# A gate store and the o-gate loads at other places in the SyncE queue (mLSTM and two MoE layers, fp32)

## The chip, the cores and the metric

The kernel runs on one core of a Trainium2 chip. The metric is the device time of one execution in microseconds (us), as the median of several runs. "Faster" and "slower" compare that time with the time of the kernel before, on the same chip.

## The reference, cut to what matters

Three layers follow each other. The first is an mLSTM with 2 batches, 8 heads, 768 steps and a head size of 40; its output feeds a top-2 mixture of 8 experts (320 to 1024 to 320), and that feeds a dense layer (320 to 2048 to 320). The change lies in the first.

```python
for t in range(S):
    m_new = np.maximum(f_gate[:, :, t] + m, i_gate[:, :, t])
    f_stab = np.exp(f_gate[:, :, t] + m - m_new)
    i_stab = np.exp(i_gate[:, :, t] - m_new)
    m = m_new
    C = f_stab * C + i_stab * np.einsum('bhd,bhe->bhde', vt, kt)
    n = f_stab * n + i_stab * kt
    h_tilde = np.einsum('bhde,bhe->bhd', C, qt)
    denom = np.maximum(np.abs(nq), 1.0)          # nq = n . q
    o = 1.0 / (1.0 + np.exp(-o_gate[:, :, t]))
    y[:, :, t] = o * h_tilde / denom
x = _moe_ref(y, ...)        # x @ w1[e], relu, @ w2[e], two experts for each row
return _moe2_ref(x, ...)    # h = x @ w_in; (h * cos(h)) @ w_out
```

## The kernel before, in words

**Tiling.** The 768 steps of each batch are cut into 6 chunks of 128 (NC = 6), so the recurrence becomes matmuls inside a chunk and a state handed from chunk to chunk. Twelve steps n = 0 to 11 follow each other in `att_step` (lines 854 to 909): n = 0 to 5 is the first batch, n = 6 to 11 the second. "qk 5" below is the load of step 5. From step 6 on the router and the experts are woven in, and from about 125 us on the program is the experts and the dense layer.

**Gates.** `gates_a(c0, c1)` (line 84) computes running sums of the gates of chunks c0 to c1-1 on VectorE, all 16 heads of both batches at once, into `g_G`, a part of the tile `g_all`. From chunk 2 on the weights of a chunk need these sums broadcast over 128 partitions. That goes through DRAM: `g_G` is stored to `GD` ("gd" in the profile, lines 102 and 103), and `load_gb(n)` (line 170) reads it back into a tile `gb`, the same 4 KB for each of 128 partitions. The sums of chunks 0 to 3 are stored once in `gates_a(2, 4)`, before step 0, and those of chunks 4 and 5 in `gates_a(4, NC)`, which step 1 calls (line 889). The load of `gb` has to wait until the store has landed.

**Loads.** All loads and stores around the change are issued by SyncE (SP), in program order, on one DMA queue; an issue waits on SP until its tile is free and its data are there, and what stands behind it in SP's program waits too. `load_qk(n)` (line 161) brings q and k with two DMAs of 40 partitions each, into one of three tiles, so qk n+3 waits until step n has used its tile up (the last user is `mk_q(n)`, lines 232 to 237, on VectorE for n = 2 and on GpSimd for n = 4 and 5). `load_kv(n)` (line 178) brings k and v, with three tiles too; its tile is free once `mm_out(n-3)` is through. `load_o(i)` (line 152) brings the o-gate of steps 2i and 2i+1 into a tile `ogt`; `tanh_o(i)` (line 156) turns it on ScalarE at the end of step i, and `mk_y` (line 315) uses it in steps 2i and 2i+1.

**Order of one step.** `att_step(n)` runs on TensorE `mm_state(n)`, `mm_out(n)`, `mm_s(n+2)` (line 239, it reads qk n+2) and the router's matmuls of the step before (`rt_a`, `rt_b`, lines 341 to 359); on VectorE `mk_state`, `mk_p(n+1)` and, for some n, `mk_q(n+1)`; then `loads(n+1)` (line 843), `mk_y(n)` with the store of the chunk's result ("xd", line 329), and on ScalarE and GpSimd `mk_w(n+2)` (line 199, it reads `gb`). `loads(n)` asks for qk n+3, gb n+3, kv n+2 and o tile n+1. For n = 2 the two `gb` tiles 4 and 5 stand at its end, since the store of their gates comes only in step 1.

Of the kernel before, what the change touches and what calls it, by code (L numbers as in the profile page):

```python
# [20 lines left out]
C = 128  # L21
NC = S // C
# [18 lines left out]
def tile_mlstm_moe_moe2(ctx, tc, qk, kv, og, gi, gf, wcat, noise, wm1, wm2, cst, out):  # L41
    nc = tc.nc
    V, A, G, T, Y = nc.vector, nc.scalar, nc.gpsimd, nc.tensor, nc.sync
# [13 lines left out]
    def psS():  # L57
        return ps.tile([128, 512], FT, name="pS", tag="S", bufs=3)

    def psM():  # L60
        return ps.tile([128, 512], FT, name="pM", tag="M", bufs=1)
# [3 lines left out]
    g_i, g_f, g_m, g_g, g_G = (g_all[0:16, i, :] for i in range(5))  # L65
# [14 lines left out]
    GD = dr.tile([NC, 16, C], FT, name="gd")  # L80
# [3 lines left out]
    def gates_a(c0, c1):  # L84
        a, z = c0 * C, c1 * C
        s = slice(a, z)
        a1 = max(a, 1)
        if a == 0:
            V.memset(g_g[:, 0:1], 0.0)
        V.tensor_tensor_scan(out=g_m[:, s], data0=g_f[:, s], data1=g_i[:, s],  # L90
                             initial=(-1e30 if a == 0 else g_m[:, a - 1:a]), op0=OP.add, op1=OP.max)
        V.tensor_tensor(out=g_g[:, a1:z], in0=g_f[:, a1:z], in1=g_m[:, a1 - 1:z - 1], op=OP.add)
        V.tensor_tensor(out=g_g[:, a1:z], in0=g_g[:, a1:z], in1=g_m[:, a1:z], op=OP.subtract)
        V.tensor_scalar(g_g[:, a1:z], g_g[:, a1:z], -110.0, None, op0=OP.max)
        for c in range(c0, c1):
            V.tensor_tensor_scan(out=g_G[:, c * C:(c + 1) * C], data0=g_r, data1=g_g[:, c * C:(c + 1) * C],
                                 initial=0.0, op0=OP.mult, op1=OP.add)
        if c0 < 2:
            A.activation(gG[:, s], g_G[:, s], AF.Copy)
        if c0 >= 2:  # L100
            d0 = 0 if c0 == 2 else c0
            Y.dma_start(GD[d0:c1].rearrange("c p t -> p c t"),
                        g_G[:, d0 * C:c1 * C].rearrange("p (c t) -> p c t", t=C))

    def gates_b(c0, c1):
        n = c1 - c0
# [26 lines left out]
    for i in range(NB):  # L133
        t = ap_.tile([128, 4, NH, C], FT, name=f"qk{i}")
# [4 lines left out]
    for i in range(2):  # L139
        t = ap_.tile([128, H, 64], FT, name=f"kb{i}")  # L140
        G.memset(t, 0.0)
        KBS.append(t)
    for i in range(2):
        t = ap_.tile([128, NH, 82], FT, name=f"st{i}")
# [7 lines left out]
    def load_o(i):  # L152
        t = OT[i] = mp.tile([128, 2, KO], FT, name="ogt", tag="wl" if i % 2 else "wh", bufs=4)
        Y.dma_start(t, og[:, 2 * i:2 * i + 2, :])
# [6 lines left out]
    def load_qk(n):  # L161
        if n >= 2 * NC:
            return
        b, c = divmod(n, NC)
        d = L[n]
        t = d["qk"] = QKS[n % NB]
        Y.dma_start(t[0:D, 0:3], qk[b, c, 0])
        Y.dma_start(t[64:64 + D, 1:4], qk[b, c, 1])

    def load_gb(n):  # L170
        if n >= 2 * NC:
            return
        b, c = divmod(n, NC)
        t = L[n]["gb"] = ap_.tile([128, H, C], FT, name="gb", bufs=3)
        Y.dma_start(t, bass.AP(tensor=GD.tensor, offset=GD.offset + (c * 16 + b * H) * C,
                               ap=[[0, 128], [C, H], [1, C]]))

    def load_kv(n):
        if n >= 2 * NC:
            return  # L180
        b, c = divmod(n, NC)
        d = L[n]
        t = ap_.tile([128, KO + H * (D + 1)], FT, name="kv", bufs=NB)
        Y.dma_start(t, kv[b, c])
        d["k"] = t[:, 0:KO].rearrange("p (h d) -> p h d", d=D)
        d["v"] = t[:, KO:].rearrange("p (h d) -> p h d", d=D + 1)
# [630 lines left out]
    load_kv(1)  # L817
    load_qk(2)
    gates_a(0, 1)
    gates_b(0, 1)  # L820
    gates_t(0, 1)
    gates_c(0, 1)
    mm_g(0)
    mk_w(0)
    mm_s(0, (0, 1))
    gates_a(1, 2)
    gates_b(1, 2)
    gates_t(1, 2)
    mm_s(0, (2, 3))
    gates_a(2, 4)  # L830
    gates_c(1, 2)
    mk_e(0)
# [10 lines left out]
    def loads(n):  # L843
        load_qk(n + 3)
        if n > 2 or n == 0:
            load_gb(n + 3)
        load_kv(n + 2)
        if n < 5:
            load_o(n + 1)
        if n == 2:  # L850
            load_gb(4)
            load_gb(5)

    def att_step(n):
        if n == 0:
            loads(0)
# [31 lines left out]
        if n == 1:  # L888
            gates_a(4, NC)
        loads(n + 1)  # L890
        if n == 2 * NC - 1:
            mk_y(n)
# [83 lines left out]
    for g in range(2, NG - 1):  # L976
        n = len(groups[g + 1][1])
# [33 lines left out]
    for q in range(3):  # L1011
        for i in range(3):
            c = 3 * q + 3 + i
# [25 lines left out]
    with tc.If(over > 0):  # L1039
# [9 lines left out]
        for b in range(B):  # L1049
            with tc.For_i(0, NC, 1) as it:  # L1050
# [4 lines left out]
                p = psM()  # L1055
# [6 lines left out]
                for e in range(E):  # L1062
                    acc = psA()
                    for f in range(8):
                        w = mp.tile([128, FW], FT, name="wr", tag="wh", bufs=4)
                        Y.dma_start(w, wm1[e, :, f, :])
                        p = psS()
# [13 lines left out]
                for f in range(16):  # L1081
                    wh, wl = W2[f // 4][:, 0, f % 4, :], W2[f // 4][:, 1, f % 4, :]
                    p = psS()
# [6 lines left out]
                t = mp.tile([128, DM], FT, name="yt", tag="yt", bufs=3)  # L1090
# [76 lines left out]
```

## Time and profile before

| what | us |
|---|---|
| median of 3 runs | 522.38 |
| lowest and highest of the 3 runs | 521.79, 523.95 |
| the profiled execution, its own time | 524.33 |
| its span in the trace | 522.1 |
| TensorE busy in that span | 489.9 (94%) |
| VectorE, ScalarE, GpSimd busy | 367.5, 326.1, 275.4 |
| DMA moved | 76.36 MB, 146 GB/s on the mean |

The span is what the trace shows of one execution, and 2.2 us of the execution's own time lie outside it. Times inside the trace count from the span's start. A share of busy time is a mean over stages that have different limits, so the stretch around the change is read by itself, and the later stages only for what they do with a shift.

### The profile page before, as it was taken

What the parts mean: (1) busy time and instruction counts of PE and PEld (TensorE: products, weight loads), DVE (VectorE), ACT (ScalarE), POOL (GpSimd) and SP (SyncE); (2) the same over time, 40 slices, a digit from 0 to 9 for tenths busy, and PEclk for the clock granted to TensorE, in tenths of its full rate; (3) what the DMA queues carried; (4) which work ended last, traced back from release to release, by engine and by line L of the source; (5) the groups of instructions that cost most, each with busy time, mean ns of one, the idle gap of its engine ahead of it and who ended that gap; (6) DMA issues with size and microseconds to landing.
All of it is one profiled execution on the core that took longest, in us unless ns stands there. A gap on an engine that the chain in (4) does not pass through costs nothing.

```text
span 522.1 us, 9011 instructions
## 1 busy us (share of the span) xinstructions
PE 489.9 (94%) x3198; PEld 470.2 (90%) x3198; DVE 367.5 (70%) x779; ACT 326.1 (62%) x695; POOL 275.4 (53%) x234
## 2 busy tenths in 40 slices
PE   4897998799999999999999997999999999999995
PEld 3796887699999999999999997989999999999995
DVE  8885387568458776868776678688956655687772
ACT  3658567355555454545555465578877777777773
POOL 6435465656846868585868687264366347300000
PEclk9999999799999999999999999999999999999998
DMA  6889785396373927391847384031021003001001
GB/s 182 255 266 268 222 269 172 119 294 261 95 285 134 334 84 268 131 352 59 325 151 254 116 312 163 28 104 26 1 64 52 1 1 102 13 2 38 1 2 43
DMA packets 25396, 76.36 MB, mean 146 GB/s; under 512 B 3872, under 2 KB 11392, under 8 KB 25344
## 3 DMA queue, kind: packets, MB, share of 16 engines
q1 hardware_dynamic: 22752, 67.11, 37.3%
q0 software_dynamic: 2592, 8.61, 5.6%
q8 instruction: 27, 0.44, 0.3%
q14 instruction: 25, 0.20, 0.1%
HBM read 66.47 MB, written 9.22 MB: 145 GB/s over the span
## 4 chain that ended last, share of the span: by engine, by line
PE 73%; DVE 12%; DMA 7%; ACT 3%; issue 3%; POOL 1%; SPq 0%; DVEq 0%; POOLq 0%; ACTq 0%
PE pS L594 34%; PE pA L603 10%; PE pA L600 10%; PE pA L599 10%; DMA qk<-qk 3%; PE pM L555 2%; PE pA L612 1%; PE pA L611 1%; DMA xgt<-xd,idxe 1%; DMA gb<-gd 1%; PE pS L310 1%; PE pA L247 1%; PE pM L355 1%; DVE c_t L717 1%; DMA gd<-g_all 1%
## 5 line engine op out<-in xcount | busy, mean ns | idle before, releaser
L587 POOL TENSOR_TENSOR wl<-wraw,wh 128x704 fp32r<-128x704 f32 x69 | 123.0, 1791 | 61.4 <-ACT wh L585 56.0
L649 DVE SCALAR_TENSOR_TENSOR hb<-pS,hb 128x384 fp32r<-128x384 f32 (+2 forms) x128 | 45.9, 390 | 45.8 <-ACT hb L646 45.0
L585 ACT ACTIVATE wh<-wraw 128x704 fp32r<-128x704 f32 x80 | 62.9, 786 | 14.3 <-PE pA L611 8.2
L594 PE MATMUL pS<-xh,wh 128*128 128x448 f32 (+1 forms) x240 | 69.5, 344 | 0.5 <-ACT xh L557 0.5
L594 PE MATMUL pS<-xh,w 128*128 128x384 f32 x288 | 66.7, 340 | 1.5 <-DVE m_t L758 1.5
L594 PE MATMUL pS<-xh,wl 128*128 128x448 f32 (+1 forms) x240 | 66.2, 330 | 0.4 <-POOL wl L587 0.4
L599 PE MATMUL pA<-wh,hb 128*128 128x320 f32 x208 | 62.3, 309 | 0.0
L600 PE MATMUL pA<-wl,hb 128*128 128x320 f32 x208 | 62.2, 309 | 0.0
L743 ACT ACTIVATE m_t<-pS,magic 128x384 f32<-128x384 f32 x64 | 37.1, 580 | 28.7 <-PE pS L594 28.1
L646 ACT ACTIVATE hb<-pS 128x448 fp32r<-128x448 f32 (+1 forms) x80 | 37.7, 472 | 25.9 <-PE pS L594 19.0
L594 PEld LDWEIGHTS pS<-xh,w 128*128 128x128 f32 x288 | 50.0, 188 | 2.8 <-DVE m_t L758 2.8
L758 DVE SCALAR_TENSOR_TENSOR m_t<-m_t,pS 128x384 f32<-128x384 f32 x64 | 35.4, 553 | 16.7 <-ACT m_t L757 16.1
L603 PE MATMUL pA<-wh,hb 128*128 128x320 f32 x208 | 44.1, 312 | 3.0 <-DVE hb L649 2.9
L594 PEld LDWEIGHTS pS<-xh,wl 128*128 128x128 f32 x240 | 43.2, 190 | 2.7 <-POOL wl L587 0.6
L744 DVE TENSOR_SCALAR m_t<-m_t 128x384 f32<-128x384 f32 x64 | 23.1, 361 | 27.3 <-ACT m_t L743 27.1
L594 PEld LDWEIGHTS pS<-xh,wh 128*128 128x128 f32 x240 | 40.9, 190 | 1.5 <-ACT xh L557 0.6
L764 POOL TENSOR_TENSOR wl<-m_t,wh 128x384 fp32r<-128x384 f32 x25 | 25.4, 1017 | 30.7 <-ACT wh L762 21.4
L594 PE MATMUL pS<-xl,wh 128*128 128x448 f32 (+1 forms) x160 | 39.7, 329 | 0.0
L600 PEld LDWEIGHTS pA<-wl,hb 128*128 128x128 f32 x208 | 38.7, 186 | 0.6
L599 PEld LDWEIGHTS pA<-wh,hb 128*128 128x128 f32 x208 | 38.6, 186 | 0.6
L546 POOL DMA_INDIRECT xgt<-xd,idx x28 | 34.3, 1224 | 7.8 <-DVE idx L519 3.2
L745 DVE SCALAR_TENSOR_TENSOR m_t<-pS,m_t 128x384 f32<-128x384 f32 x64 | 35.7, 558 | 2.2
(201 smaller groups left out, 1243.4 us busy)
## 6 DMA issues: line engine op xcount, KB each, us to landing
wraw<-wm SPq DMA_DIRECT2D x36, 704.0 KB
raw<-wm SPq DMA_DIRECT2D x16, 704.0 KB
qk<-qk SPq DMA_DIRECT2D x24, 240.0 KB
gb<-gd SPq DMA_DIRECT2D x10, 512.0 KB
kv<-kv SPq DMA_DIRECT2D x12, 324.0 KB
yd<-yt SPq DMA_DIRECT2D x22, 160.0 KB
wraw<-wm SPq DMA_DIRECT2D x8, 352.0 KB
ogt<-og SPq DMA_DIRECT2D x6, 320.0 KB
```

Source lines behind the costliest of these rows:

```text
L546: G.indirect_dma_start(out=t[:n, :], out_offset=None, in_=XD[0:S, :] if g < 2 else XD[:, :], in_offset=bass.IndirectOffsetOnAxis(ap=(idxe ...
L585: A.activation(wh, raw[:, f, :], AF.Copy)
L587: eng.tensor_tensor(out=wl, in0=raw[:, f, :], in1=wh.bitcast(FT), op=OP.subtract)
L594: T.matmul(p[:, :n], w[:, 128 * k:128 * k + 128], x[:, m, :], start=(i == 0), stop=(i == 7))
L599: T.matmul(a[:n, :DM], hh[:, s], wh[:, KW:], start=first, stop=False)
L600: T.matmul(a[:n, :DM], hh[:, s], wl[:, KW:], start=False, stop=False)
L603: T.matmul(a[:n, :DM], hl[:, s], wh[:, KW:], start=False, stop=last)
L646: A.activation(hh[:, :n], p[:, :n], AF.Relu)
L649: V.scalar_tensor_tensor(out=hb[:, o:o + z - a], in0=p[:, a:z], scalar=0.0, in1=hh[:, a:z].bitcast(FT), op0=OP.max, op1=OP.subtract)
L743: A.activation(t, m["p"], AF.Identity, bias=magic, scale=0.5 / PI)
L745: V.scalar_tensor_tensor(out=t, in0=m["p"], scalar=0.5 / PI, in1=t, op0=OP.mult, op1=OP.subtract)
L758: V.scalar_tensor_tensor(out=s, in0=s, scalar=1.0, in1=m["p"], op0=OP.subtract, op1=OP.mult)
```

## The change

The store of the gates of chunks 4 and 5 leaves `gates_a` and becomes a function of its own, `gates_d`. `gates_a(2, 4)` still stores chunks 0 to 3 where it did. The other store now stands in `loads(2)`, behind the issues of qk 5, an o tile and kv 4, and right ahead of the loads of gb 4 and gb 5. The o tiles move as well: o tile n is asked for in `loads(n)` and no longer in `loads(n-1)`, and it stands ahead of the kv tile and not behind it.

```diff
         if c0 < 2:
             A.activation(gG[:, s], g_G[:, s], AF.Copy)
-        if c0 >= 2:
-            d0 = 0 if c0 == 2 else c0
-            Y.dma_start(GD[d0:c1].rearrange("c p t -> p c t"),
-                        g_G[:, d0 * C:c1 * C].rearrange("p (c t) -> p c t", t=C))
+        if c0 == 2:
+            gates_d(0, c1)
+
+    def gates_d(c0, c1):
+        Y.dma_start(GD[c0:c1].rearrange("c p t -> p c t"),
+                    g_G[:, c0 * C:c1 * C].rearrange("p (c t) -> p c t", t=C))
...
         load_qk(n + 3)
         if n > 2 or n == 0:
             load_gb(n + 3)
+        if 0 < n < NC:
+            load_o(n)
         load_kv(n + 2)
-        if n < 5:
-            load_o(n + 1)
         if n == 2:
+            gates_d(4, NC)
             load_gb(4)
             load_gb(5)
```

No instruction is added or taken away. Each of the lines stands for one DMA issue on SP (two for a qk).

## Rows read from the trace of the kernel before

**Rows 1.** Chain that ended last, 0 to 75 us: start us, length us, what
```profile
14.13 1.80 DMA gd<-g_all
...
29.07 2.11 DMA gd<-g_all
...
31.24 6.16 DMA gb<-gd
...
43.43 7.77 DMA qk<-qk
```

**Rows 2.** Timelines of ScalarE and TensorE, 13 to 72 us: start, length, what, [idle before]
```profile
37.48 2.45 ACT L209 ACTIVATE wt<-gb,tok 128x128 f32<-128x128 f32 x8 [1.37 <-DMA gb<-gd]
...
42.28 0.94 PE L355 MATMUL pM<-wc,xTt 128*128 128x128 f32 x6 [1.23 <-ACT xTt L348]
...
51.34 1.15 PE L247 MATMUL pA<-qk 128*128 128x256 f32 x2 [2.01 <-DMA qk<-qk]
```

**Rows 3.** Busy time by stretch, 50 to 56 us: PE, PEld, DVE, ACT, POOL, PEclk, DMA share, GB/s
```profile
50.00:52.00 2.00, 0.66 (x2) 0.60 (x3) 1.38 (x4) 2.00 (x9) 0.64 (x1) 0.85 0.96 338
52.00:54.00 2.00, 2.00 (x10) 1.81 (x9) 1.05 (x2) 0.72 (x2) 0.70 (x2) 0.50 1.03 278
54.00:56.00 2.00, 2.00 (x13) 1.86 (x12) 0.00 (x0) 0.00 (x0) 0.66 (x1) 0.80 0.89 239
```

**Rows 4.** The page: busy tenths of TensorE in 40 slices of 13 us
```profile
PE   4897998799999999999999997999999999999995
```

**Rows 5.** Timeline of SP's issues: start, length, line, what
```profile
6.19 0.30 SPq L168 DMA_DIRECT2D qk<-qk  x1
...
29.07 0.34 SPq L102 DMA_DIRECT2D gd<-g_all  x1
29.50 0.31 SPq L167 DMA_DIRECT2D qk<-qk  x1
...
31.24 0.81 SPq L175 DMA_DIRECT2D gb<-gd  x2
```

**Rows 6.** Busy time by stretch, 12 to 36 us, columns as in rows 3
```profile
12.00:14.00 2.00, 1.75 (x4) 0.85 (x3) 1.90 (x5) 0.00 (x0) 0.74 (x1) 1.00 0.66 229
...
26.00:28.00 2.00, 2.00 (x18) 1.95 (x17) 1.90 (x4) 0.49 (x1) 0.69 (x3) 1.00 0.62 190
28.00:30.00 2.00, 2.00 (x19) 1.95 (x18) 1.79 (x6) 1.11 (x5) 0.45 (x1) 1.00 0.52 182
...
34.00:36.00 2.00, 1.73 (x17) 1.54 (x16) 1.50 (x4) 0.34 (x3) 0.46 (x1) 1.00 1.02 375
```

**Rows 7.** DMA issues of the whole run: out<-in, engine, count, KB each
```profile
qk<-qk SPq DMA_DIRECT2D x24, 240.0 KB
gb<-gd SPq DMA_DIRECT2D x10, 512.0 KB
kv<-kv SPq DMA_DIRECT2D x12, 324.0 KB
...
ogt<-og SPq DMA_DIRECT2D x6, 320.0 KB
```

**Rows 8.** Timelines of VectorE and TensorE, step 1: who frees qk 5's and kv 4's tiles
```profile
24.89 0.68 DVE L237 TENSOR_TENSOR qtt<-qk,get 128x512 f32<-128x512 f32 x1
25.48 1.21 DVE L90 TENSOR_TENSOR_SCAN g_all<-g_all 16x256 f32<-16x256 f32 x1
...
28.09 0.95 DVE L96 TENSOR_TENSOR_SCAN g_all<-g_r,g_all 16x128 f32<-16x128 f32 x2
...
27.08 0.61 PE L310 MATMUL pS<-kv,ppt 128*128 128x82 f32 x4
```

**Rows 9.** Timeline of ScalarE: when o tiles 3 and 5 are used, and the idle after tile 4
```profile
45.88 0.72 ACT L157 ACTIVATE ogt<-ogt 128x640 f32<-128x640 f32 x1
...
56.92 0.49 ACT L348 ACTIVATE xTt<-pM 128x384 f32<-128x384 f32 x1 [4.21 <-PE pM L346]
...
61.11 0.73 ACT L157 ACTIVATE ogt<-ogt 128x640 f32<-128x640 f32 x1
```

## The prediction

> **What bounds the kernel now.** I read the chain that ended last first, then the waits of the engines in the stretch that the change touches, then the queue. In the chain, DMA holds four long pieces between 14 and 52 us [rows 1]: two gate stores, the load of gb 4, which lands at 31.24 + 6.16 = 37.40 us, and qk 7, which lands at 43.43 + 7.77 = 51.20 us. The reader is to see that a store of 16 KB needs 2.11 us and one of 32 KB 1.80 us: a small transfer costs its fixed way there and back, about 1.8 us, and hardly its bytes. The loads of 480 to 512 KB take 6 to 8 us; that is not their bytes but what stands ahead of them.
>
> Two of these landings stop engines [rows 2]. ScalarE waits 1.37 us for gb 4, and as its queue runs in order the router's xTt of step 2 comes late behind it: TensorE waits 1.23 us at 42.28. Then TensorE waits 2.01 us for qk 7 at 51.34. Behind that second wait the granted clock falls from 2.4 to 1.2 GHz [rows 3]: the means 0.85, 0.50 and 0.80 over three stretches of 2 us lose 2 x (0.15 + 0.50 + 0.20) = 1.7 us of clock. Together these are 1.23 + 2.01 + 1.7 = 4.9 us, all that a better order of loads could win here. From 125 us on (slice 10) TensorE is busy 9 tenths in nearly every slice [rows 4]: whatever the first stage gains or loses is handed through to the end, with nothing that would take it up.
>
> **Is there room in the queue?** At 26 to 30 us the DMA engines are busy only 0.62 and 0.52 [rows 6], while qk 5 could already be under way: its tile is free at 24.89 + 0.68 = 25.57 and its issue stands at 29.50, behind the gate store, which waits for VectorE's scans until 28.09 + 0.95 = 29.04 [rows 5, 8]. This is what the change goes after. But the share is a mean over 16 engines. At 12 to 14 us the last thing asked for was qk 2, at 6.19 [rows 5], and the 2 x 229 = 458 kB moved then are less than its two halves of 240 KB, 492 kB [rows 6, 7]. So a qk alone keeps 0.66 of the engines busy, 10.6 of 16, and moves 229 GB/s, where gb and kv in the stretch from 34 us get 375. A 0.6 with a qk ahead is therefore a queue whose fullest engines do not rest.
>
> The Trainium skill says the same in two places of "DMA: Bandwidth & Descriptors": under "Why a DMA increments its semaphore by 16 and not by 1", that a DMA is spread over the largest number of engines up to 16 that divides its outer dimension, by which 40 partitions give 10; and under "Queues, rings and completion order", that each engine takes its descriptors in ring order. By that rule the moved store cannot pass the loads that are now ahead of it on those ten engines, and it speaks against this change. The 0.66 agrees with the 10; what the rule makes of the time is the main case below, and the time without it is rival 1.
>
> **The change part by part.**
>
> *The price of each load in the queue.* Of the 1.80 us I give half, 0.9, to the way before the data and half to the way back; no row splits it, so the ends are 0 and 1.8. Then qk 5 (issued 29.50), kv 4, an o tile and gb 4 are served from 30.4 to 36.5, 6.1 us. At 375 GB/s gb (524 kB) is 1.40, kv (332 kB) 0.88, an o tile (328 kB) 0.87; qk is left with 2.95. Its lower bound is 492 kB at 229 GB/s, 2.15.
>
> *The o tiles one step later.* Up to `loads(2)` one o tile less has gone in, so the queue reaches qk 5 0.87 us earlier: 29.5 and not 30.4. From then on each `loads(n)` up to 4 holds one o tile as before, so the lead neither grows nor shrinks; at `loads(5)` the extra tile comes back and costs 0.87 us of the queue. Who uses the tiles: tanh 2 has them long before. Tile 4 has 4.21 us of idle ScalarE behind it [rows 9], so a late one costs nothing unless it is over 4.2 us late. Tiles 3 and 5 are rival 3. The kv tiles now stand 0.87 us later within their step; their users, GpSimd's kb and the next step's matmuls, come a step or more later, and I cost this at nothing, with 0.5 us as the other end.
>
> *The loads ahead of the store.* On SP qk 5 can issue at 25.6, the o tile at 26.3, kv 4 when `mm_out(1)` has let its tile go at 27.08 + 0.61 = 27.7 [rows 8]. All three are issued by about 28.1, so the store still leaves SP at 29.07, as soon as the scans are through; SP's order costs it nothing. The queue does. That a transfer waits for the fullest of its engines I take from gb 4, whose 6.16 us [rows 1] are over what its bytes need by the time of the loads ahead. So the store is served behind 29.5 + 2.95 (qk 5) + 0.87 (o) + 0.88 (kv 4) = 34.2, and with its way back it lands at 35.2 instead of 31.18. The ends are 34.3 and 36.1 by the split of the 1.8 us.
>
> *What waits for the store.* gb 4 leaves SP 0.06 us after the landing, as before (31.18 to 31.24) [rows 1], and nothing is ahead of it in the queue, so it lands 1.80 + 1.40 = 3.2 us after its issue, at 38.45 against 37.40: **+1.05 us**, with +0.1 and +1.9 as ends. Behind it on SP wait gb 5, the store of step 1's result and qk 6, gb 6 and so on. These lose nothing of their own: gb 4 and gb 5 fill the engines until about 39, and qk 6 issues at 36.4.
>
> *The same in terms of the queue.* But for the store itself it is empty from 34.2 to 35.25 + 0.9 = 36.1, some 1.9 us in which nobody asks for anything, and it has 0.87 us less to carry: everything behind, up to qk 8, is 1.9 - 0.87 = +1.0 us. Before, the round trip of the store was covered by qk 5, kv 4 and the o tile issued behind it; now that cover has gone ahead of it.
>
> *To the end.* ScalarE's wait for gb 4 becomes 1.37 + 1.05 = 2.4 us, and TensorE's at 42.28 becomes 2.3. qk 7 is issued a little later, which its place in the queue hides, and lands at 52.2. TensorE was there at 51.34 - 2.01 = 49.33, would now be at 49.33 + 1.05 = 50.4 and wait 1.8 us, so step 5 starts at 52.3 and not 51.34. **Sum: +1.0 us**, 525.3 against the profiled execution's 524.33. That execution was 1.95 us above the median of the runs; on the median the sum gives 522.38 + 1.0 = **523.4 us**.
>
> **The rivals.**
>
> *1. The store is not held up.* If the engines that it uses are not those that are behind, it lands near 31.2 as before. gb 4 then follows kv 4 without a hole: 34.2 + 1.4 + 0.9 = 36.5, 0.9 us earlier, and qk 7 is 0.9 us earlier too. That is 521.5, and if the shorter waits spare the clock, another 1.7 us: 519.8. For it: the mean share of 0.52 to 0.62 at 26 to 30 us. Against: at that share qk's engines are full, and gb 4 took 6.16 us behind qk 5.
>
> *2. The clock falls elsewhere.* TensorE's first wait grows to 2.3 us, over the 2.01 us behind which the clock fell; the second shrinks to 1.8. If it falls behind the first, the slow stretch of 1.7 us lies in step 4, where TensorE has those 1.8 us to wait for qk 7 anyway, and step 5 runs at 2.4 GHz: +1.0 - 1.7 = -0.7, and as qk 9 is late by the extra o tile, some of it is lost again: 521.7 to 522.4. For it: the lengths of the waits. Against: the wait of 1.23 us cost no clock, and one example does not tell where between 1.23 and 2.01 it turns.
>
> *3. An o tile comes too late (slower).* tanh 5 stands in ScalarE's queue at 61.11 [rows 9], in a stretch where ScalarE itself is on the chain; with the shift it is wanted at 62.1. Behind qk 7 (52.2) come gb 7, o 4, kv 6, a result store (160 KB, 0.44), qk 8, gb 8 and o 5: 1.40 + 0.87 + 0.88 + 0.44 + 2.95 + 1.40 + 0.87 = 8.8, landing at 61.0. But from gb 4 to qk 7 the same prices give 11.3 us where the trace has 13.8 [rows 1], a factor of 1.22; with it o 5 lands at 62.9 and tanh 5 waits 0.8 us, with the upper end of gb 4 as much as 1.7. Everything behind it shifts: +1.0 + 0.8 to 1.7, or 524.2 to 525.1. It decides from the point where o 5 lands after 62.1; tile 3 (wanted at 46.9, landing at 45.5 to 47.1) has the same trouble but qk 7's wait hides it.
>
> *4. The parts cancel.* The saved o tile and the hole in the queue are equal (the split of the 1.8 us at its low end): 522.4.
>
> **How the numbers follow.** Main case 0.42; rival 1 0.10; rival 2 0.23; rival 3 0.15; rival 4 0.10. What a measurement of this kernel can tell from no change is about 0.5%, 2.6 us. Of the cases only the better half of rival 1 is faster by that (0.05); rival 3's upper end together with the main case's (+1.9) is slower by it (0.12). The rest, 0.83, stays within. The range takes in rivals 2, 3 and 4 and the lesser half of rival 1, and no more: 521.4 to 525.1.
>
> **What would show it.** Right: the two gate DMAs of the chain at 14 and 29 us become one of about 1.8 and one of about 6 us; SP's issue of gb 4 moves to about 35.2; gb 4's own time shrinks from 6.16 to about 3.2; ScalarE's wait for it is over 2 us; the DMA share falls below 0.5 around 35 us; TensorE reaches step 5 about 1 us later. Wrong: a gate store of under 3 us, gb 4 landing before 37.4, or a wait of ScalarE for an o tile of over 1 us. The prediction is also wrong if the later stages take up or add to the shift, which rows 4 gives no sign of.

## The result: 2.6 us slower

The kernel after takes 525.03 us on the median of 11 runs, the kernel before 522.45 on the median of 11: a ratio of 1.0052, with a 95% interval from 1.0034 to 1.0070, or +2.6 us with +1.8 to +3.7. A second series of the same kernel gave 525.2 us and 1.0059 [1.0036, 1.0082]. The forecast was 523.4 us (+1.0), with a range up to 525.1. So the direction held and the size did not: the loss is two and a half times the sum. The measured time lies just inside the range, in the part of it that only rival 3 reaches. The profiled execution after took 526.23 us with a span of 524.2; that of before took 1.9 us less, 524.33.

Line numbers are those of the kernel whose trace is shown; in the kernel after they are two or three higher than before. First the chain of work that ended last, 0 to 75 us, its DMA pieces (start, length, what). It answers [rows 1]:

```profile
14.12 2.04 DMA gd<-g_all
17.02 7.15 DMA qk<-qk
...
44.64 8.48 DMA gb<-gd
53.18 4.81 DMA kv<-kv
...
59.98 5.71 DMA xd<-xt
```

Neither the second gate store nor gb 4 is in it any more: from 24.3 to 44.6 us it runs through the engines, and from there to 65.7 us it names DMA pieces. But the chain's releasers are inferred, and not all of these pieces can be real waits. The kv piece ends at 57.99 us, when the packets of kv 7 were still arriving (the last ended at 60.86); and the instruction that the chain puts behind it and behind the result store (xd), ScalarE's `den` in line 323, reads a product of TensorE and neither of the two. So what follows goes by the waits of the engines. First SP's issues, which answer [rows 5]:

```profile
25.67 0.30 SPq L169 DMA_DIRECT2D qk<-qk  x1
26.02 0.33 SPq L170 DMA_DIRECT2D qk<-qk  x1
26.40 0.35 SPq L156 DMA_DIRECT2D ogt<-og  x1
28.80 0.35 SPq L186 DMA_DIRECT2D kv<-kv  x1
29.25 0.37 SPq L104 DMA_DIRECT2D gd<-g_all  x1
34.46 0.80 SPq L177 DMA_DIRECT2D gb<-gd  x2
...
36.45 0.31 SPq L169 DMA_DIRECT2D qk<-qk  x1
```

The store leaves at 29.25, and what waits for it, gb 4, at 34.46: 5.2 us for a store of 16 KB that took 2.11. Busy time by stretch (columns as in [rows 3]) shows what the DMA engines do meanwhile; it answers [rows 6]:

```profile
30.00:32.00 2.00, 2.00 (x17) 1.92 (x17) 1.60 (x5) 1.98 (x9) 0.37 (x1) 1.00 0.84 253
32.00:34.00 2.00, 2.00 (x18) 1.92 (x18) 1.90 (x4) 1.98 (x6) 1.53 (x3) 1.00 0.36 137
34.00:36.00 2.00, 2.00 (x17) 1.75 (x15) 1.94 (x5) 0.96 (x2) 1.27 (x3) 1.00 0.12 49
36.00:38.00 2.00, 1.73 (x17) 1.66 (x16) 1.29 (x5) 0.45 (x3) 0.00 (x0) 1.00 0.83 326
38.00:40.00 2.00, 2.00 (x17) 1.90 (x16) 1.20 (x4) 1.74 (x6) 0.33 (x1) 1.00 0.64 229
```

At 34 to 36 us the share is 0.12, where the kernel before has 1.02 [rows 6]: the hole is there. From 36 to 40 us it is 0.83 and 0.64, although both gb tiles have been asked for: the queue doesn't come back at full share. Last, ScalarE and TensorE, the lines that answer [rows 2, 9] (start, length, what, [idle before]); ScalarE:

```profile
38.26 2.45 ACT L211 ACTIVATE wt<-gb,tok 128x128 f32<-128x128 f32 x8 [1.08 <-DMA gb<-gd]
...
47.18 0.74 ACT L159 ACTIVATE ogt<-ogt 128x640 f32<-128x640 f32 x1 [0.42 <-DMA ogt<-og]
...
54.39 0.74 ACT L159 ACTIVATE ogt<-ogt 128x640 f32<-128x640 f32 x1 [1.05 <-DMA ogt<-og]
...
61.20 0.74 ACT L159 ACTIVATE ogt<-ogt 128x640 f32<-128x640 f32 x1 [0.71 <-DMA ogt<-og]
```

and TensorE:

```profile
24.30 0.67 PE L249 MATMUL pA<-qk 128*128 128x256 f32 x2 [1.57 <-DMA qk<-qk]
...
43.06 0.94 PE L357 MATMUL pM<-wc,xTt 128*128 128x128 f32 x6 [0.94 <-ACT xTt L350]
...
52.27 0.67 PE L249 MATMUL pA<-qk 128*128 128x256 f32 x2 [1.70 <-DMA qk<-qk]
...
58.91 0.67 PE L249 MATMUL pA<-qk 128*128 128x256 f32 x2 [0.32 <-DMA qk<-qk]
```

ScalarE's wait for gb 4 has not grown (1.08 us against 1.37), but three o tiles are waited for that no line of before waits for, by up to 1.05 us (the second profile of the kernel after, below, has none of these three waits). Step 5 starts at 52.27 and not at 51.34.

When a load landed can also be worked out from the trace's packets, as each kind of load has packets of a size of its own. These are the ends of the last packet, in us, in two profiles of each kernel:

```
load     before            after             later, means
gb 4     36.50   37.31     37.44   37.99     +0.8
gb 5     38.24   38.97     40.56   41.28     +2.3
qk 7     50.14   50.26     51.07   51.33     +1.0
qk 8     56.73   56.74     58.00   58.11     +1.3
qk 9     61.95   62.47     64.16   64.11     +1.9
kv 8     64.01   64.52     66.21   66.16     +1.9
```

The reader is to see that the loads drift apart behind qk 7, where the forecast stopped counting.

### The profile page after: what moved, and what is told of

The parts are those of the page before. It is cut to its first block, busy times and chain, and to the rows that moved or that the text cites. A ratio compares the mean times of both kernels' runs of the same rounds, so it can differ in the third digit from the quotient of the medians.

```text
span 524.2 us, 9011 instructions
## 1 busy us (share of the span) xinstructions
PE 490.2 (94%) x3198; PEld 470.3 (90%) x3198; DVE 367.2 (70%) x779; ACT 326.5 (62%) x695; POOL 274.9 (52%) x234
## 4 chain that ended last, share of the span: by engine, by line
PE 75%; DVE 11%; DMA 8%; issue 3%; ACT 1%; SPq 0%; POOL 0%; DVEq 0%; ACTq 0%; POOLq 0%
PE pS L596 35%; PE pA L605 10%; PE pA L601 10%; PE pA L602 10%; PE pM L557 2%; DMA gb<-gd 2%; DMA qk<-qk 1%; PE pA L614 1%; PE pA L613 1%; PE pS L312 1%; DMA xgt<-xd,idxe 1%; DMA xd<-xt 1%; PE pM L357 1%; PE pA L249 1%; DMA kv<-kv 1%
## 5 line engine op out<-in xcount | busy, mean ns | idle before, releaser
L596 PEld LDWEIGHTS pS<-xh,wl 128*128 128x128 f32 x240 | 43.6, 192 | 2.7 <-POOL wl L589 0.6
```

What stands on the lines that cost most here:

```text
L596: T.matmul(p[:, :n], w[:, 128 * k:128 * k + 128], x[:, m, :], start=(i == 0), stop=(i == 7))
```

## The experiments

**Two series of the unchanged kernels**, for the scatter.

> The kernel before once more, unchanged: what two sets of runs of one kernel differ by, and a second profile of it. Every theory: ratio 1.000, with an interval of 0.002 to each side. Clock theory (the profiled pair differs mostly by how long TensorE ran at 1.2 GHz around 92 to 102 us, which changes from run to run): this profile need not have the low stretch at 51 to 55 us, and the one at 92 us is 6.8 or 10.2 us long by chance.

> The changed kernel once more: a second profile, and runs beside the others of this call. Queue theory with my sum: ratio 1.002. Sum too small, clock (its longer waits make TensorE run at 1.2 GHz more often, which the sum left out): ratio 1.004 to 1.006 as first measured, mean granted clock of its runs about 0.0025 below that of the kernel before, and the first 76 us alone are longer by about 1 us only when a low stretch falls into them.

Before again: 522.49 us, ratio 0.9995 [0.9978, 1.0011]. After again: 525.2 us, 1.0059 [1.0036, 1.0082]. Their profiles start alike (step 1 at 23.77 us in both), and in that of after the hole is nearly empty. One row each, before again and then after again:

```profile
34.00:36.00 2.00, 1.73 (x14) 1.46 (x14) 1.82 (x3) 0.59 (x2) 0.93 (x2) 1.00 1.00 302
```

```profile
34.00:36.00 2.00, 1.73 (x14) 1.45 (x14) 1.82 (x3) 0.60 (x2) 0.93 (x2) 1.00 0.02 6
...
46.00:48.00 2.00, 2.00 (x9) 1.82 (x9) 1.72 (x4) 2.00 (x6) 1.17 (x2) 0.50 0.81 272
48.00:50.00 2.00, 2.00 (x9) 1.82 (x8) 0.69 (x1) 1.28 (x3) 0.73 (x2) 0.50 0.97 229
```

In this execution of after TensorE's clock was granted at 1.2 GHz (0.50) from about 45 to 52 us, where the other had 2.4. The low stretch of [rows 3], in turn, is absent from the second profile of before. So a single profile carries about 1 to 2 us of its own. A mark behind the first stage shows it: the router's matmul that waits for `r_os`, here before again:

```profile
68.93 0.91 PE L355 MATMUL pM<-wc,xTt 128*128 128x128 f32 x6 [0.51 <-DVE r_os L421]
...
77.69 0.70 PE L247 MATMUL pA<-qk 128*128 128x256 f32 x2 [0.33 <-DVE ppt L256]
```

and here after:

```profile
70.56 0.91 PE L357 MATMUL pM<-wc,xTt 128*128 128x128 f32 x6 [0.51 <-DVE r_os L423]
...
79.31 0.70 PE L249 MATMUL pA<-qk 128*128 128x256 f32 x2 [0.32 <-DVE ppt L258]
```

The mark stands at 70.46 and 68.93 in the two profiles of before, at 70.56 and 71.58 in those of after; from it to the next line shown it is 8.75 to 8.77 us in all four. They don't run alike all the way: from the mark to the end of the span it is 451.7 and 452.6 us in the two profiles of before, 453.6 and 451.6 in those of after. The first pair, 2.1 us apart at the end, is only 0.1 apart at the mark, and most of the rest comes in between 85 and 105 us, where the clock was low for 10.2 us in the first profile of after and for 6.8 us in the other three (3.4 us more at half the clock are 1.7 us). On the means of the two profiles the kernel after is 1.4 us later at the mark and 1.9 us later at the end. So most of what the change does is done by 70 us, and what comes behind it goes at least in part with the clock of the single profile.

**Can the store pass the loads on a queue of its own?** The second store is issued by ScalarE (e3); all else as in the kernel after.

```diff
     def gates_d(c0, c1):
-        Y.dma_start(GD[c0:c1]...
+        (A if c0 else Y).dma_start(GD[c0:c1]...
```

> The changed kernel with the second store issued by ScalarE, so on a queue of its own, the loads of qk 5, o 2 and kv 4 still ahead of gb 4. Queue theory: the store leaves at about 29 and lands near 31.2 and not 34.4, gb 4 follows kv 4 without a hole and lands at 36.5 to 37; ratio 0.998 to 1.001. Rival (the store is slow for another reason, its memory write or the load on the engines as a whole): it still lands 4 to 5 us after its issue, and the time stays at 1.004 to 1.006.

525.65 us, 1.0048 [1.0029, 1.0066]: the whole loss is still there. The chain, and ScalarE's issue:

```profile
29.21 5.92 DMA gd<-g_all
35.15 3.61 DMA gb<-gd
```

```profile
29.21 0.36 ACTq L104 DMA_DIRECT2D gd<-g_all  x1
```

The store leaves 0.14 us after VectorE's scans and with nothing ahead of it on its queue, and yet needs 5.92 us. Rival 1 falls: what holds the store up is the work on the DMA engines, not its place in SP's queue.

The Trainium skill says in "DMA: Bandwidth & Descriptors", "Issuing engines are not separate DMA queues", that DMAs of different issuing engines interleave on the same 16 engines; the 5.92 us agree that another issuing engine buys nothing here. The same page of the Trainium skill, under "Queues, rings and completion order", has each engine take turns between queue rows packet by packet, by which the small store could have gone ahead of the backlog; the row shows that it did not.

**How much stands ahead of the store.** Three kernels that move the store alone, or put less or more ahead of it.

```diff
# e5: the store right behind qk 5, o tiles as after
         load_qk(n + 3)
+        if n == 2:
+            gates_d(4, NC)
...
         if n == 2:
-            gates_d(4, NC)
             load_gb(4)
```

```diff
# e11: as e5, o tiles as before;   e1: the store as after, o tiles as before
-        if 0 < n < NC:
-            load_o(n)
         load_kv(n + 2)
+        if n < 5:
+            load_o(n + 1)
```

> The changed kernel with the store behind qk 5 alone; the o tile and kv 4 are asked for behind the store, so they cover its round trip again. Queue theory (what costs is the hole while nothing is asked for): the store lands about 1.7 us earlier than in the changed kernel (32 to 33 us), no hole, gb 4 lands at 37 to 37.5, ratio 0.999 to 1.002. Rival (what costs is the store's delay behind qk 5, or the late o tiles): nearly all of the loss stays, ratio 1.004 to 1.006.

> The store behind qk 5 alone, kv 4 and o tile 3 behind the store, and the o tiles asked for early as in the kernel before. Queue theory: qk 5 is in the queue from 25.6 us on, the store lands at 33 to 34, its round trip is covered by kv 4 and o 3 (1.75 us), gb 4 lands at 37.4 to 38.5; ratio 0.999 to 1.002, and the difference to the same with late o tiles (1.0024) is what late o tiles cost: 0.000 to 0.002. Rival (any delay of the store is lost in full): gb 4 lands 2 us or more later, ratio 1.004 or more.

> The store alone is moved: it stands behind qk 5, kv 4 and o tile 3, and the o tiles are asked for as in the kernel before. Queue theory (the store waits on the fullest engines behind the loads, and its round trip leaves a hole): the store lands 0.9 us later than in the changed kernel, at about 35.3 us or later, gb 4 at about 39, and with no o tile saved the time is +1.9 us or a little more over before (ratio 1.004 or more). Rival, late o tiles (the loss comes from tanh waiting for its tile): the o tiles are early again, so the loss is gone, ratio 1.000 to 1.001.

Behind qk 5 alone: 523.35 us, 1.0024 [1.0000, 1.0048], and with the o tiles of before 523.86 us, 1.0027 [1.0013, 1.0041]; about half of the loss is gone (with intervals that overlap that of the kernel after), and when the o tiles come makes no difference that shows. Behind qk 5, kv 4 and o tile 3: 526.83 us, 1.0077 [1.0049, 1.0105], +4.0 us. The chain of e5 and then that of e1:

```profile
29.97 4.09 DMA gd<-g_all
34.07 3.67 DMA gb<-gd
```

```profile
30.22 6.56 DMA gd<-g_all
...
36.85 3.79 DMA gb<-gd
```

The store lands later the more is ahead of it. In e11, with one o tile more ahead than in e5, it took 6.21 us (28.74 to 34.95), longer than in the kernel after, and still only 1.4 us are lost: there kv 4 and an o tile stand behind it. So the store's own length does not set the loss; whether loads stand behind it counts as well. In e1 the hole moves later, to 36 to 38 us:

```profile
36.00:38.00 2.00, 1.73 (x16) 1.53 (x15) 1.30 (x5) 0.45 (x3) 0.00 (x0) 1.00 0.07 24
```

As e1 has the o tiles of before and the largest loss, a loss of this size needs no late o tiles.

**The o tiles alone**: the store where it was, the o tiles as after.

```diff
# e2, against the kernel before (the store stays in gates_a)
+        if 0 < n < NC:
+            load_o(n)
         load_kv(n + 2)
-        if n < 5:
-            load_o(n + 1)
```

> The o tiles alone are moved, one step later and ahead of kv; the store stays in front of qk 5 as in the kernel before. Queue theory: one o tile less ahead of gb 4 and qk 7, no hole, so gb 4 lands at about 36.5 and the time is -0.9 us to 0 (ratio 0.998 to 1.000). Late o tiles: tanh 3, 4 and 5 wait as in the changed kernel (0.42, 1.05 and 0.71 us) and the time is +1 to +2.6 us (ratio 1.002 to 1.005).

523.17 us, 1.0014 [0.9995, 1.0033]: no gain. The forecast had the queue reach qk 5 earlier by one o tile, 0.87 us. SP's issues say why it doesn't:

```profile
29.37 0.34 SPq L104 DMA_DIRECT2D gd<-g_all  x1
29.80 0.31 SPq L169 DMA_DIRECT2D qk<-qk  x1
```

With the store in front, qk 5 leaves SP at 29.80 whatever lies before it in the queue; the tile saved only makes the share before that smaller (0.61 from 24 to 32 us, where the two profiles of before have 0.70 and 0.62).

**Ten engines for a qk.** The two halves of a qk are split into 32 and 8 partitions, in the kernel before and in the kernel after, to see whether a transfer over all 16 engines takes the hole's cause away.

```diff
-        Y.dma_start(t[0:D, 0:3], qk[b, c, 0])
-        Y.dma_start(t[64:64 + D, 1:4], qk[b, c, 1])
+        for r0, r1 in ((0, 32), (32, D)):
+            Y.dma_start(t[r0:r1, 0:3], qk[b, c, 0, r0:r1])
+        for r0, r1 in ((0, 32), (32, D)):
+            Y.dma_start(t[64 + r0:64 + r1, 1:4], qk[b, c, 1, r0:r1])
```

> The kernel before with each load of 40 partitions issued as two, of 32 and of 8, the same bytes at the same places. Ten-engine theory (the queue is bound by the 10.6 engines that a qk keeps busy): with 32 partitions spread over all engines and 8 over half of them the fullest engine has 3 rows in place of 4 of each half, a qk costs about 2.2 us in place of 2.95, and qk 7 lands 2 to 3.5 us earlier; TensorE's wait for it goes. Ratio 0.992 to 0.996. Rival (the queue is bound by bytes or by memory as a whole): landings stay, four issues on SP cost 0.3 us each, ratio 1.000 to 1.003.

> The changed kernel with the same split of the qk loads. Ten-engine theory: the store's wait behind qk 5 shrinks from 5.2 us to about 4.3 or less and the queue has room, so the loss against the kernel of the same split without the change shrinks from 2.5 us to 0 to 1.5; ratio against the kernel before 0.992 to 0.998. Rival (the store itself is slow): the loss stays, and the ratio is 0.005 above that of the split alone.

530.71 us, 1.0167 [1.0144, 1.0189], and 531.85 us, 1.0179 [1.0160, 1.0198]. The expectation failed: the split alone costs 8.7 us. From 13 to 14 us in the kernel before, the packets under way are those of a qk alone, 10 at a time: a share of 0.65 and 184 GB/s. In the split kernel before it is so from 8 to 9 us, with 16 at a time: 0.95 and 172 GB/s. The row of 8 to 10 us, in whose second half packets of an o tile join:

```profile
8.00:10.00 2.00, 2.00 (x9) 1.96 (x10) 1.83 (x7) 1.07 (x5) 0.00 (x0) 1.00 1.01 182
```

So the ten-engine reading of the share holds (10 packets under way, and the split fills the share), but not what the expectation made of it: six more engines moved no more bytes. A share says nothing on bytes. Why the split kernel is slower was not found. The loss between the two is 1.1 us, with about 1.5 to either side; with a queue as slow as this the pair doesn't weigh much.

**TensorE's clock.** Matmuls that nobody reads are to keep TensorE busy over the waits of steps 3 to 5, in both kernels; first 6 ahead of `rt_b` in step 3 and 9 at the head of step 5, then 5 ahead of `rt_b` in step 3 and 7 behind `rt_b` in step 4.

```diff
+    def warm(n, m):
+        for _ in range(m):
+            T.matmul(L[n]["po"][:, 384:512], ident, ident, start=True, stop=True, ...)
...
# e9, e10
         mm_state(n)
+        if n == 5:
+            warm(4, 9)
...
+        if n == 3:
+            warm(3, 6)        # e12, e13: warm(3, 5)
         if n:
             rt_b(n - 1, psS if n == 9 else None)
+        if n == 4:            # e12, e13 alone
+            warm(4, 7)
```

> The kernel before with 15 matmuls added that nobody reads: 6 on TensorE where it waits in step 3 for the router's xTt, 9 at the head of step 5 where it waits for qk 7, some 0.2 us each at 2.4 GHz, so about 1.2 and 1.8 us of its waits are filled. Clock theory (low stretches follow these waits and cost time): no stretch at 1.2 GHz between 40 and 60 us, ratio 0.996 to 1.000. Rival (the low stretches lie under the waits for DMA and cost nothing): ratio 1.000 to 1.002.

> The changed kernel with the same 15 matmuls. Clock theory: what the change costs beyond the late landings is clock, so its loss against the kernel before with the same matmuls falls from 2.5 us to 1.0 us, ratio 1.000 to 1.003, and the mean granted clock of its runs comes up to that of the kernel before. Rival (all of the loss is late landings): the loss stays, ratio 0.005 above that of the kernel before with the same matmuls.

> The kernel before with 12 matmuls added that nobody reads, each of two passes of about 0.125 us: 5 in step 3 ahead of the router's matmuls that wait for xTt (1.25 us), 7 in step 4 behind the router's matmuls, where TensorE is about to wait for qk 7 (1.75 us), and ahead of that step's mk_y, so that they wait for nothing. Clock theory: no stretch at 1.2 GHz between 40 and 60 us, mean granted clock up; ratio 0.997 to 1.000. Rival (a low stretch here lies under waits and costs nothing): ratio 1.000 to 1.002.

> The changed kernel with the same 12 matmuls in the same places. Clock theory: the loss against the kernel before with the same matmuls falls from 2.5 us to about 1.0 to 1.3 us, what the late landings alone give. Rival (all of it is late landings, of which my sum had less than half): the loss stays at 2.0 to 3.0 us.

The first pair was misplaced: 526.57 us, 1.0073 [1.0047, 1.0099], and 530.56, 1.0158 [1.0125, 1.0190]. TensorE's line in the kernel before with it:

```profile
51.73 2.25 PE L856 MATMUL pS<-ident 128*128 128x128 f32 x18 [1.98 <-DVE xt L327]
```

The added matmuls wait themselves, for `mk_y`, and so lie behind the wait and not in it. The pair (4.0 us between the two) decides nothing. The second pair waits for nothing: 523.57 us, 1.0023 [1.0004, 1.0043], and 526.92, 1.0075 [1.0050, 1.0101], a loss of 3.3 us between them on the medians (2.7 by the ratios), with about 1.7 to either side (the half widths of the two intervals, added in squares). If the clock between 40 and 60 us were what lies between +1.0 and +2.6, the pair should have lost about 1.0; in both profiles the mean there is 1.00. But the clock fell elsewhere in the second: behind a wait of 2.07 us for qk 3, ahead of the moved store. Its SP issues show what that did:

```profile
25.52 0.30 SPq L169 DMA_DIRECT2D qk<-qk  x1
...
30.95 0.35 SPq L186 DMA_DIRECT2D kv<-kv  x1
31.40 0.37 SPq L104 DMA_DIRECT2D gd<-g_all  x1
36.58 0.80 SPq L177 DMA_DIRECT2D gb<-gd  x2
```

VectorE's scans ended at 28.51, yet the store left at 31.40: it stands on SP behind kv 4, and kv 4 waits until TensorE has used its tile up, at 30.92. In the pair's kernel before, step 1 was late as well (24.06 us), and there the store left at 28.51, 0.03 us after the scans.

**Without o tile 5.** The load of o tile 5 and its tanh are left out of both kernels (tile 4 is used in its place), to see whether the extra tile at `loads(5)` is a term of the loss.

```diff
-        if n < 5:            # e14; e15: if 0 < n < NC  ->  0 < n < NC - 1
+        if n < 4:
             load_o(n + 1)
...
-    for i in range(1, NC):
+    for i in range(1, NC - 1):
         put(i, tanh_o, i)
+    put(5, lambda: OT.setdefault(5, OT[4]))
```

> The kernel before without o tile 5: its load and its tanh are left out, and steps 10 and 11 use tile 4 as step 8 and 9 left it, so 256 rows get another gate. This is the base of the next run. Both theories: one load of 320 KB and one tanh of 0.7 us less where ScalarE is on the chain, ratio 0.996 to 1.000.

> The changed kernel with the same left out: no o tile 5, so the tile that comes back to the queue at the load of step 5 is gone, and no tanh can wait for it. Theory of added terms (the loss is 1.0 us of late landings plus 0.9 to 1.5 us for the extra o tile ahead of kv 7 and qk 9 and the late tanh 5): the loss against the run before this one falls from 2.5 us to 0.5 to 1.3 us. Rival (the store's hole alone costs the 2.5 us, since behind it the queue starts slowly): the loss stays at 2.0 to 3.0 us.

523.50 us, 1.0024 [1.0007, 1.0041], and 524.91, 1.0051 [1.0024, 1.0078]: between them 1.4 us, with about 1.7 to either side, instead of 2.6. But the edit does less than it was meant to: e15 asks for its tiles in `loads(1)` to `loads(4)`, so the extra tile is not gone, it comes back at `loads(4)` in place of `loads(5)`. The ends of the last packets say so: in e15 qk 7 is 0.5 us later than in e14, and qk 8, qk 9 and kv 8 are 1.7 us later. What the pair takes out is the wait of tanh 5. Its profiles are the cleanest pair there is (step 1 starts at 23.62 and 23.61, and neither has a low clock from 40 to 60 us): the mark of the router stands at 67.12 and 68.20, +1.1 us, of which 0.6 are there at the start of step 5 (50.29 and 50.87) and the rest behind a late qk 8 (TensorE waits 0.33 us for it at 57.51). A smaller loss fits the wait of tanh 5 as a term of it, but the interval holds 2.6 too. Why leaving a load out of the kernel before makes it 0.7 us slower on the medians (1.3 by the ratio) and not faster was not found.

**All kernels beside each other.** The share of the DMA engines by stretch, 8 us each and then 10, and the work they had done by 40 us (8 us times the sum of the first two). The loss is the ratio's; "clock lost" is, on the mean of each kernel's runs, one less the granted clock, times the run's time.

```
kernel                         24-32  32-40  40-50   done by 40   loss us   clock lost us
before, profile 1 / 2          0.70   1.02   0.89    13.8         0         6.0 (103 runs)
                               0.62   1.01   0.85    13.0
o tiles alone (e2)             0.61   0.98   0.81    12.7         0.7       6.2
store behind qk 5 (e5)         0.71   0.78   0.96    11.9         1.3       6.1
the same, o as before (e11)    0.84   0.72   0.96    12.5         1.4       6.8
after, profile 1 / 2           0.84   0.49   0.96    10.6         2.7       7.2
                               0.84   0.52   0.96    10.9         3.1       8.8
store from ScalarE (e3)        0.84   0.60   0.94    11.5         2.5       6.6
behind qk 5, kv 4, o 3 (e1)    0.89   0.49   0.94    11.0         4.0       7.8
```

Where less work was done by 40 us, more was lost, with e1 the exception. No kernel here beats the kernel before.

## Why the prediction was right in its sign and wrong in its size

**The store: right.** 5.2 us in both profiles of after (29.25 to 34.46, 29.89 to 35.16), forecast as 6.1. It is served behind qk 5, the o tile and kv 4; e5, e11 and e1 show that it follows what stands ahead, and e3 that a queue of its own doesn't help. The first gate store, now the only one in the chain, took 2.04 us against 1.80.

**The hole: right in kind, too small in size.** The forecast gave it 1.9 us less 0.87 for the saved o tile. The table has the DMA engines do 13.4 us of work by 40 us in the kernel before and 10.75 in the kernel after, on the means: 2.65 us less. Two terms were off. The saved o tile gives nothing where qk 5's issue sets the pace (e2). And the hole doesn't end when gb 4 is asked for: gb 5, issued with it, lands 2.3 us later than before, not 1. Half way, between 40 and 50 us, the kernel after wins some of it back: the share is 0.96 against 0.89 and 0.85, or 10 x 0.09 = 0.9 us. That slack of the kernel before was not in the forecast either; the errors nearly cancel at qk 7, which lands 1.0 us later, as forecast, but by luck. One reading of the forecast was off without changing its sum: in the stretch of [rows 6] from which it took 229 GB/s for a qk alone, kv packets were under way until about 13 us; a qk alone moved 184 GB/s.

**gb 4 and the engines' waits: only partly.** gb 4's own time fell from 6.16 to about 3.7, as forecast, and its last packet ended 0.8 us later against 1.05. But ScalarE's wait for it was to become 2.4 us; it is 1.08 and 2.28 in the profiles of after and 1.37 and 2.15 in those of before, and TensorE's for xTt 0.94 and 2.14 against 1.23 and 2.00. With step 1 starting alike (the second profiles) the xTt matmul stands at 43.70 and not at 43.55, 0.15 us later. Here the forecast lay at its lower end (+0.1): gb 4 did not carry the loss, the queue behind it did.

**Step 5: right, in part by luck.** 52.27 against the forecast's 52.3, but in a profile that starts step 1 a microsecond late (24.30 and not 23.23). Before again, which starts it at 23.77 and has no low stretch there either, begins step 5 at 51.47: 0.8 us earlier.

**The step that failed: the sum ended at step 5.** The forecast found that the extra tile "comes back" at `loads(5)` and "costs 0.87 us of the queue", and then did not add it to its main case; it stood in rival 3, as an alternative with a chance of 0.15. It is not an alternative: qk 9 and kv 8 land 1.9 us later, which is about qk 7's 1.0 and the tile's 0.87. What it costs is read at tanh 5, which the mark at 70 us follows by 9.35 or 9.36 us in all four profiles. The result above has tanh 5 of the first profile of after (61.20), [rows 9] that of before; here are before again and after again:

```profile
59.58 0.72 ACT L157 ACTIVATE ogt<-ogt 128x640 f32<-128x640 f32 x1
```

```profile
62.23 0.73 ACT L159 ACTIVATE ogt<-ogt 128x640 f32<-128x640 f32 x1
```

Before again and the first profile of after have no low clock between 20 and 90 us, so they can be compared. In the second of these step 5 starts 0.8 us later (51.47, 52.27), tanh 5 starts 1.6 us later (59.58, 61.20) and has waited 0.71 us for its tile, and the mark is 1.6 us later (68.93, 70.56). So in this pair, where the clock is high, the term that was left out is worth 0.8 us, the price that rival 3 had put on tanh 5's wait. In after again tanh 5 does not wait: the low stretch from 45 to 52 us has held ScalarE back until the tile was there. The tile and a low stretch ahead of it do not add up at this place; the later of the two counts. Rival 3 was written down as 524.2 to 525.1 and holds the measured time; but its upper half came from a gb 4 that is 1.9 us late, where the two profiles of after have 0.8, so that part is luck.

Of the two profiles of after only the first waits for tiles 3 and 4 (0.42 and 1.05 us). The 1.05 us is one of the forecast's signs of being wrong, but it costs nothing: ScalarE idles another 1.07 us behind it. The users of kv, costed at nothing, can be held too; GpSimd's kb of kv 7 in the kernel after (the profile names a result store as the releaser, which kb does not read; kv 7's last packet ended at 60.86, 2.0 us later than before):

```profile
62.55 0.72 POOL L231 TENSOR_TENSOR kb<-kv,kdec 128x320 f32<-128x320 f32 x1 [1.36 <-DMA xd<-xt]
```

Before, the same line stands at 61.88 with no wait; that this one costs time is not shown. Nor do the runs without a profile show the tile's term: with the tiles alone moved e2 loses 0.7 us with 1.0 to either side, and e5 less e11, the same store with late and early tiles, is -0.2 us with 1.5 to either side.

**A step that fails at times: "SP's order costs it nothing".** The store was to leave with the end of the scans. In the second profile of after it does (29.89, scans until 29.86). In the first, kv 4 waits until 28.80 and the store leaves 0.6 us behind the scans; in e13 it is 2.9 us. The forecast took the time at which `mm_out(1)` frees kv 4's tile from one profile, 27.7. It hangs on when qk 3 lands, and TensorE's start of step 1 spread from 23.23 to 24.82 over the profiles of the kernels without the split. Before, a late step 1 did not touch the store. How often it happens in runs that were not profiled is not known.

**Rival 4, the parts cancel: no.** The interval of the loss begins at +1.8 us.

**Rival 2, the clock: not as written.** It had the clock spare time, and took the length of a wait for what decides. Before again waited 2.00 us at 43.55 and e15 2.20 us at 43.63, and no low stretch followed; after again waited 2.14 us at 43.70, and one followed from 45.3 to 52.1 us. The first profile of after indeed has no low stretch in step 5. Behind 90 us the means of 20 us differ as well. Before, then after:

```profile
90.00:110.00 20.00, 14.35 (x103) 13.70 (x104) 10.14 (x25) 7.73 (x19) 11.46 (x10) 0.83 0.52 160
```

```profile
90.00:110.00 20.00, 14.66 (x95) 14.20 (x95) 8.40 (x22) 7.65 (x18) 11.53 (x10) 0.74 0.51 159
```

Over all runs the kernel after had a mean granted clock of 0.9852 (17 runs) and the kernel before 0.9885 (103): 7.75 and 6.0 us lost, 1.75 more. That is a bound, since some of it falls into waits.

**What stays open.** +1.0 at qk 7, 0.87 for the tile and up to 1.75 of clock make more than 2.6, so they can't all count in full; at tanh 5 the tile and the clock were seen to cover each other. Taking the clock off the losses of the table leaves 0.9 for after (mean of both series), 2.2 for e1 and 0.5 for e2, close to the expected prices, but 1.9 for e3, twice its price; and e13 loses 3.3 us with a high clock in the stretch in question. Among the runs of one kernel time and granted clock go closely together in some (the lower the clock the longer the time, with a correlation of -0.88 in the 7 runs of e1, -0.80 in the 12 of e5) and hardly in others (-0.28 in the kernel before, -0.02 in the kernel after). So of the gap of 1.6 us the profiles show 0.8 for the tile where the clock is high; where the rest comes from, and how the executions without a profile divide between the tile and the clock, was not settled.

**The later stages: not settled.** Between 85 and 105 us the four profiles part by up to 1.9 us, the one with 10.2 us of low clock losing most; from 110 us to the end they keep their distances within 0.3 us, so what is lost by then is handed through. TensorE's row of the page is that of [rows 4] digit for digit, but slices of 13 us can't show a shift of 2 us.

## What to carry to other kernels

A small store that a load waits for needs transfers queued behind it, to cover its round trip, and none ahead: put it in front of the loads, for its time is that of the backlog, whether SP or ScalarE issues it. An idle-looking DMA share is only room if the transfers under way could use it, and a full one is only speed if its bytes say so. Go on adding costs until the last tile that was moved has been used, and treat what comes on top as a term and not as a rival; and don't read a loss of 1 us from one profile of a kernel.

## What the hardware showed that was not expected

- A store of 16 KB on ScalarE's otherwise empty queue took 5.92 us while SP's queue had a backlog, no less than on SP's own (5.2); its first packet came 2.0 us after the issue, and 0.85 us without a backlog.
- A qk split into transfers of 32 and 8 partitions kept the DMA engines busy at a share of 0.95 and moved 172 GB/s (e6, 8 to 9 us), where the unsplit one moved 184 at 0.65 (before, 13 to 14 us). Two issues of the split qk took SP 0.68 to 2.08 us; most unsplit ones took 0.30 to 0.35 each, single ones up to 1.64.
- After the hole the queue ran from 36 to 40 us at shares of 0.64 to 0.87 in the two profiles of after (0.91 and 1.02 in e3), with work asked for, where it ran at 1.03 to 1.07 without a hole.
- The clock fell behind a wait of 2.01 us in one profile of the kernel before, in the other (with 0.86 us at that place) not there at all; waits of 2.00 us near 43.6 us in that other profile and of 2.20 in e15 were followed by no low stretch; the same kernel's profiles differ by up to 1.5 us at 70 us.
